# Moving one more batch of output transposes from TensorE to DMA, with a new order of loads and a new rule for the fillers

## The chip, the core and the metric

The kernel runs on one core of one Trainium2 chip. The metric is the device time of that core in microseconds (us), from the first to the last instruction, taken over several executions. Beside each kernel the kernel before was run on the same chip in the same rounds.

PE is the matrix engine (TensorE), ACT is ScalarE, DVE is VectorE, POOL is GpSimd. SP is the engine that issues most of the loads. The granted clock is the share of PE's full clock that it was given in a stretch; 1.00 is full. "PE stands" means that it is idle and waits.

## The reference

The first half is attention with a forget gate; the second half is two linear layers with a SiLU between them.

```python
# q, k, v: (8, 8, 576, 64)   f: (8, 8, 576)   all float32
scores = scale * np.matmul(q, k.transpose(0, 1, 3, 2))
cum = np.cumsum(np.log(np.clip(f, 0.0001, 1.0)), axis=-1)
decay = cum[:, :, :, None] - cum[:, :, None, :]
scores = np.where(causal, -1e9, scores + decay)     # causal: above the diagonal
attn = softmax(scores)                              # max, exp, sum, as usual
x = np.matmul(attn, v) -> (4608, 512)               # 4608 tokens, heads side by side
h = x @ w_in                                        # 512 x 2048
out = (h * sigmoid(h)) @ w_out                      # 2048 x 512
```

## The kernel before

The first 128 tokens of each batch ("heads" of the sequence) are done in an opening phase, batch by batch. Then a loop over 16 pairs of head pairs does the other 448 tokens of each batch. The attention runs ahead; between its steps PE is fed with pieces of the two layers for tokens whose attention is done. A piece of the first layer is `m1_chunk` (line L568, output `hp`), a piece of the second is `m2_part` (L613, output `po`). Between them ACT takes a tanh of `hp` (`th`), and DVE multiplies the two (`gt`, L577): that frees the buffer of `hp`, and `gt` is the input of the second layer. The scores are `sc` (L460). The program sets the order of the instructions on each engine: in the trace of this kernel POOL issues the loads in the program's order, w_out's first two pieces at 25.31 us behind the conversion of v of batch 4 (24.31).

The outputs of PE live in two pools. The scores have one of their own; everything else, `hp`, `po`, the attention outputs `dn` and the transposes `tx`, shares four buffers with the tag "big":

```python
psc = ctx.enter_context(tc.tile_pool(name="psc", bufs=2, space=bass.MemoryType.PSUM))
pbig = ctx.enter_context(tc.tile_pool(name="pbig", bufs=4, space=bass.MemoryType.PSUM))
```

`back(m)` turns (transposes) the attention output of pair-of-pairs m, so that it can be an input of the first layer. It does this by DMA, or by seven transposes on PE and two copies on DVE:

```python
BY_DMA = [2 * 2 <= m < NQ - 1 for m in range(NQ)]        # NQ = 16
def back(m):
    ...
    if BY_DMA[m]:
        nc.sync.dma_start_transpose(out=xr..., in_=xq[:, 0 : 2 * NR, ...])
        nc.sync.dma_start_transpose(out=xt..., in_=xq[:, 2 * NR, ...])
        return
    tx = pbig.tile([P, NGR, P], BF16, name="tx", tag="big")
    for c in range(NGR):                                 # NGR = 7
        nc.tensor.transpose(tx[:, c, :], xq[:, c, ...], ident_bf[:, :])
    nc.vector.tensor_copy(out=xr, in_=...)
    nc.vector.tensor_copy(out=xt, in_=...)
```

`step()` picks the next filler. It compares how far the first layer is in its group of tokens (f1) with how far the second layer is in the group before (f2), and mostly alternates:

```python
f1 = M1[a][1] / NFC
f2 = (c - sum(M2_OF[:g2])) / M2_OF[g2]
want = 3 - at["last"] if abs(f1 - f2) < 0.15 else (1 if f1 < f2 else 2)
if want == at["last"] and at["row"] >= 2 and abs(f1 - f2) < 0.25:
    want = 3 - want
```

The loads of the opening phase are issued by POOL, those of the pair loop by SP. After SP's loads of the first pairs come the cast (on POOL) and the DMA transpose of q and k of pair 0, `qkT`, which the first scores of the pair loop need:

```python
load_qk(2); load_v(0, 2); load_v(0, 3); load_qk(3)       # SP
for n in range(2):
    cast_qk(n)                                           # POOL
    transposes(n)                                        # SP, by DMA: qkT
```

SP's queue has a gate in front of these loads: a tiny DMA into `junk` (the `after(...)` of the kernel), which waits until the second piece of w_out has landed.

The pair loop, cut:

```python
for m in range(NQ):
    scores(n, 0); scores(n, 1); prepare(n)
    slot(piece, 2)                                       # fillers, second layer first
    if m > 0: back(m - 1); ...
    scores(n, 2); scores(n + 1, 0); prepare(n + 1); slot(piece, 2)
    scores(n + 1, 1); scores(n + 1, 2); slot(piece, 2)
    attend(n); attend(n + 1); slot(..., 1)
```

The softmax here doesn't subtract the row's maximum and nothing guards it: scores larger than these inputs give would overflow.

## Time and profile before

| | before |
|---|---|
| median of the runs | 350.6 us (349.71 to 350.83) |
| span of the profiled run | 348.5 us |
| PE busy | 333.4 us, 96% |
| ACT busy | 216.8 us, 62% |
| PE waits for loads of w_out / q | 2.6 us / 1.6 us |
| PE waits for DVE to free a buffer (`po` on `gt`) | 0.9 us |
| PE transposes of attention outputs | 35, in five streams of seven (pair indices 0 to 3, and the last) |

PE is the bound, so the reader looks for two things: what takes PE's time, and where PE stands. The prediction below shows those lines. In the groups of instructions (busy us, mean ns of one, idle before it and what ended most of that):

```profile
L549 PE MATMUL tx<-ident_bf,xr 128*128 128x128 bf16 x35 | 2.8, 219 | 0.2 <-DVE gt L577 0.2
```

In the timeline of PE, start, length, instruction: the first scores of the pair loop start at 62.80 us without a wait.

```profile
62.80 0.40 PE L460 MATMUL sc<-qkT 64*128 64x128 bf16 x8
...
63.35 1.04 PE L613 MATMUL po<-w_out_bf,gt 128*128 128x512 bf16 x4
```

### The profile page before, as it was taken

How to read it: one execution, taken by the hardware profiler on the slowest of the kernel's cores; microseconds unless marked ns; L12 is line 12 of the kernel's file. 1: busy time of each engine (PE TensorE's matmuls, PEld its weight loads, DVE VectorE, ACT ScalarE, POOL GpSimd, SP SyncE). 2: the span in 40 equal slices, each digit the busy share in tenths (PEclk: the TensorE clock that was granted, in tenths of full speed). 3: DMA queues.
4: the chain of work that ended last, by engine and by line, in shares of the span. 5: the costliest groups of instructions: out<-in, count | busy, mean ns of one | idle time of the engine just before them, and what ended most of it. 6: DMA issues, size and time to landing. Idle time of an engine off the chain costs nothing.

```text
span 348.5 us, 8844 instructions
## 1 busy us (share of the span) xinstructions
PE 333.4 (96%) x3520; PEld 199.4 (57%) x3567; DVE 179.4 (51%) x389; ACT 216.8 (62%) x401; POOL 130.0 (37%) x227
## 2 busy tenths in 40 slices
PE   8989969999899999999999999999999999999995
PEld 3644545567656566565665666756656565555664
DVE  4763815366556555645546554645645463444340
ACT  5855624867766758759667585785865934545341
POOL 8997325447271263245235028313620000010011
PEclk9999999999999999999999999999999999999999
DMA  8999999999999398799799789679952100011012
GB/s 155 193 203 207 213 202 184 219 199 188 190 168 187 96 185 165 177 208 163 163 221 137 169 165 194 158 153 197 174 104 58 52 32 30 32 53 40 30 60 62
DMA packets 141497, 50.44 MB, mean 145 GB/s; under 512 B 132368, under 2 KB 138768, under 8 KB 141456
## 3 DMA queue, kind: packets, MB, share of 16 engines
q1 hardware_dynamic: 131440, 32.70, 53.5%
q0 software_dynamic: 9856, 17.04, 20.5%
q8 instruction: 28, 0.46, 0.6%
q10 hardware_dynamic: 160, 0.13, 0.1%
q14 instruction: 13, 0.11, 0.1%
HBM read 36.85 MB, written 9.44 MB: 133 GB/s over the span
## 4 chain that ended last, share of the span: by engine, by line
PE 83%; DMA 6%; ACT 4%; POOL 3%; issue 3%; DVE 1%; ACTq 0%
PE po L613 34%; PE hp L568 29%; PE sc L460 7%; DMA w_out_bf<-in_moe_w_out_dram 6%; PE dn L507 5%; PE dn L516 3%; PE tp L286 2%; PE wm L232 1%; ACT u L464 1%; ACT ut L476 1%; ACT osb L623 1%; POOL qkb L131 1%; PE tx L549 1%; ACT th L576 1%; POOL w_in_bf L190 0%
## 5 line engine op out<-in xcount | busy, mean ns | idle before, releaser
L576 ACT ACTIVATE th<-hp 128x384 bf16<-128x384 f32 (+2 forms) x208 | 95.7, 481 | 88.2 <-PE hp L568 86.3
L577 DVE SCALAR_TENSOR_TENSOR gt<-th,hp 128x384 bf16<-128x384 bf16 (+2 forms) x208 | 105.5, 522 | 82.1 <-ACT th L576 79.0
L613 PE MATMUL po<-w_out_bf,gt 128*128 128x512 bf16 (+1 forms) x550 | 138.7, 373 | 6.7 <-DMA w_out_bf<-in_moe_w_out_dram 2.6
L568 PE MATMUL hp<-x,w_in_bf 128*128 128x384 bf16 (+2 forms) x700 | 129.0, 321 | 0.5
L568 PEld LDWEIGHTS <-w_in_bf 128*128 128x128 bf16 x832 | 78.1, 98 | 53.8 <-issue 1.6
L613 PEld LDWEIGHTS <-gt 128*128 128x128 bf16 x592 | 55.1, 98 | 53.1 <-issue 6.3
L592 POOL DMA_DIRECT2D out_dram<-osb x38 | 21.0, 553 | 170.1 <-ACT osb L623 130.6
L464 ACT ACTIVATE u<-sc 128x1024 bf16<-128x1024 f32 (+1 forms) x96 | 75.2, 822 | 11.9 <-PE sc L460 11.7
L414 POOL TENSOR_TENSOR vp<-vf,w_bf 128x520 bf16<-128x520 f32 (+1 forms) x32 | 35.0, 1100 | 21.2 <-DMA vf<-in_v_dram 14.8
L469 DVE TENSOR_TENSOR u<-u,tri 128x768 bf16<-128x768 bf16 x32 | 20.1, 628 | 24.7 <-ACT u L464 24.7
L623 ACT ACTIVATE osb<-po 128x512 f32<-128x512 f32 (+1 forms) x37 | 22.1, 598 | 14.4 <-PE po L613 14.2
L460 PE MATMUL sc<-qkT 64*128 64x128 bf16 (+1 forms) x640 | 26.5, 207 | 0.1
L460 PEld LDWEIGHTS <-qkT 64*128 64x128 bf16 x640 | 18.2, 94 | 11.8 <-issue 9.3
L483 DVE TENSOR_TENSOR ut<-ut,trit 128x128 bf16<-128x128 bf16 x32 | 8.5, 265 | 30.7 <-ACT ut L476 30.7
L476 ACT ACTIVATE ut<-sc 128x640 bf16<-128x640 f32 x32 | 23.2, 726 | 0.0
L507 PEld LDWEIGHTS <-u 128*128 128x128 bf16 x576 | 20.8, 97 | 3.6 <-issue 0.3
L507 PE MATMUL dn<-vp,u 128*128 128x65 bf16 x384 | 21.8, 193 | 0.0
L525 DVE TENSOR_TENSOR xr<-dn,rec 128x448 bf16<-128x448 f32 x32 | 20.0, 624 | 1.1
L507 PE MATMUL dn<-v,u 128*128 128x65 bf16 x192 | 19.8, 193 | 0.2 <-DVE gt L577 0.2
L400 POOL CAST qkb<-qf 128x384 bf16<-128x384 f32 x32 | 16.2, 508 | 9.2 <-DMA qf<-in_q_dram 8.4
L400 POOL CAST qkb<-kf 128x384 bf16<-128x384 f32 x32 | 18.7, 583 | 2.2 <-DMA kf<-in_k_dram 2.2
L568 PE MATMUL hp<-xt,w_in_bf 128*128 128x256 bf16 x128 | 17.7, 273 | 0.1
(68 smaller groups left out, 204.6 us busy)
## 6 DMA issues: line engine op xcount, KB each, us to landing
out_dram<-osb POOLq DMA_DIRECT2D x32, 256.0 KB, 3.2
vf<-in_v_dram SPq DMA_DIRECT2D x26, 256.0 KB, 4.9
qf<-in_q_dram SPq DMA_DIRECT2D x64, 96.0 KB, 3.0
kf<-in_k_dram SPq DMA_DIRECT2D x64, 96.0 KB, 2.9
w_in_bf<-in_moe_w_in_dram POOLq DMA_DIRECT2D x4, 512.0 KB, 7.2
w_out_bf<-in_moe_w_out_dram POOLq DMA_DIRECT2D x4, 512.0 KB, 10.3
vf<-in_v_dram POOLq DMA_DIRECT2D x6, 256.0 KB, 7.4
qkb<-in_q_dram POOLq DMA_DIRECT2D x8, 128.0 KB, 5.3
```

The lines of the kernel that those rows point to most:

```text
L400: nc.gpsimd.tensor_copy(out=t2[:, c0 : c0 + NR, :].rearrange("p c x -> p (c x)"), in_=t[:, :, :, :].rearrange("p c h d -> p (c h d)"),)
L414: nc.gpsimd.tensor_tensor(out=vbf[b][r, c, :, :], in0=vst[b][c][r, :, :], in1=w_bf[r, c + 1, b * H : (b + 1) * H, None].to_broadcast([n, H ...
L460: nc.tensor.matmul(sc[:, i, o : o + q1 - q0], lhsT=kt, rhs=t[r, q0:q1], start=True, stop=True)
L464: nc.scalar.activation(out=u[:, :, c * SM : c * SM + w], in_=sc[:, :, 0:w], func=ACT.Exp, scale=scale)
L476: nc.scalar.activation(out=ut[:, :, 0:3:2, :].rearrange("p k i t -> p i k t"), in_=sc[:, :, T0 : T0 + (NM + 1) * ST].rearrange("p i (k t) ...
L507: nc.tensor.matmul(dn[:, i * NR + c - 1, :], lhsT=u[:, i, o : o + P], rhs=vals(kb, i), start=(kb == 0), stop=(kb == c),)
L568: nc.tensor.matmul(hp[:, :], lhsT=w_in_bf[:, cc, fc * P : (fc + 1) * P], rhs=xcols(g, cc), start=(cc == 0), stop=(cc == NCC - 1),)
L576: nc.scalar.activation(out=th[:, :], in_=hp[:, :], func=ACT.Tanh, scale=0.5)
L577: nc.vector.scalar_tensor_tensor(out=gt[:, fc, :], in0=th[:, :], scalar=1.0, in1=hp[:, :], op0=ALU.add, op1=ALU.mult,)
L592: q_.dma_start(out=dst, in_=src)
L613: nc.tensor.matmul(po[:, :], lhsT=gt[:, fc, tb * P : (tb + 1) * P], rhs=w_out_bf[:, fc, m0:m1], start=(fc == 0), stop=(fc == NFC - 1),)
L623: nc.scalar.activation(out=osb[:, :], in_=po[:, :], func=ACT.Copy, scale=0.5)
```

## The change

The intent is to take the transposes of the second batch's outputs from PE to DMA (BY_DMA from m = 2 instead of 4). With them come a rule for the fillers and a new order of POOL's loads in two places.

```diff
-    BY_DMA = [2 * 2 <= m < NQ - 1 for m in range(NQ)]
+    BY_DMA = [2 <= m < NQ - 1 for m in range(NQ)]
@@ step()
+            if sum(M2_OF[: g2 + 1]) - c <= 2:
+                want = 1
@@ first part of the load order
     load_qk0(4)
+    load_qk0(5)
+    load_w_in(2)
+    load_w_in(3)
     load_v0(4)
-    load_w_in(2)
-    load_qk0(5)
     load_v0(5)
-    load_w_in(3)
@@ second part of the load order
-    convert_v0(4)
     load_w_out(0)
     load_w_out(1)
+    convert_v0(4)
     convert_v0(5)
-    load_qk0(6)
-    load_v0(6)
-    load_qk0(7)
-    load_v0(7)
     load_w_out(2)
     load_w_out(3)
+    load_qk0(6)
+    load_qk0(7)
+    load_v0(6)
+    load_v0(7)
```

Below, "the rule" is the second of these edits, "the first hunk" and "the second hunk" are the two parts of the load order.

## The prediction

> **What bounds the kernel now.** I read the page first, then the waits of the matrix engine, then stretches of 10 us, then single stretches in order of time.
>
> From the page: busy time of the matrix engine (PE), and two rows of the span in 40 slices (tenths of a slice busy):
>
> ```profile
> span 348.5 us, 8844 instructions
> PE 333.4 (96%) x3520; PEld 199.4 (57%) x3567; DVE 179.4 (51%) x389; ACT 216.8 (62%) x401; POOL 130.0 (37%) x227
> ...
> PE   8989969999899999999999999999999999999995
> ...
> DMA  8999999999999398799799789679952100011012
> ```
>
> PE is the bound: 15.1 us of it idle, and the last slice (the final eviction and store) alone holds about 4. DMA is full from the start to slice 12, some 110 us, then has gaps. So before 110 us PE runs beside a second resource with no reserve.
>
> The waits that PE met (us in total, times, longest):
>
> ```profile
> PE po L613 <- DMA w_out_bf<-in_moe_w_out_dram: 2.6, 2, 1.8
> PE tp L286 <- DMA qkb<-in_q_dram: 1.6, 1, 1.6
> ...
> PE po L613 <- DVE gt L577: 0.9, 1, 0.9
> ```
>
> Only these three are worth more than 0.5 us, apart from the start. The first two are loads that come late. The stretches show where (columns: stretch, its length, then PE busy; last but one is the DMA share):
>
> ```profile
> 20.00:30.00 10.00, 8.32 (x97) 4.34 (x98) 5.58 (x9) 4.02 (x8) 8.35 (x17) 1.00 1.17 210
> 30.00:40.00 10.00, 9.86 (x75) 5.35 (x75) 6.99 (x13) 8.53 (x16) 5.79 (x8) 1.00 1.22 216
> 40.00:50.00 10.00, 7.25 (x43) 4.11 (x43) 3.03 (x8) 2.81 (x7) 2.47 (x5) 1.00 1.05 190
> ```
>
> From 110 to 340 us PE is busy 227.4 of 230 us: there the only gain is less work for PE. The third wait is the one I looked at longest, because it tells what the change's reordering will do. The timeline of PE, then of ScalarE (ACT), then of VectorE (DVE), at 90 to 94 us (start, length, instruction):
>
> ```profile
> 89.86 0.34 PE L460 MATMUL sc<-qkT,kT 64*128 64x384 bf16 x2
> ...
> 90.38 1.92 PE L568 MATMUL hp<-x,w_in_bf 128*128 128x256 bf16 x16
> 93.25 1.02 PE L613 MATMUL po<-w_out_bf,gt 128*128 128x512 bf16 x4 [0.95 <-DVE gt L577]
> ```
>
> ```profile
> 90.50 1.37 ACT L464 ACTIVATE u<-sc 128x1024 bf16<-128x1024 f32 x2
> 91.67 0.80 ACT L476 ACTIVATE ut<-sc 128x640 bf16<-128x640 f32 x1
> 92.25 1.42 ACT L576 ACTIVATE th<-hp 128x256 bf16<-128x256 f32 x4
> ```
>
> ```profile
> 92.77 1.41 DVE L577 SCALAR_TENSOR_TENSOR gt<-th,hp 128x256 bf16<-128x256 bf16 x4
> ```
>
> PE did score matmuls, then four first-layer chunks (16 matmuls) in 1.92 us. ACT had to do the exponentials of those scores before the four tanh, so the first tanh began at 92.25 and the first product on DVE ended at 93.2. The four chunks sat in the four buffers of the pool "big"; the next output needed a fifth, and PE stood for 0.95 us. So: more first-layer chunks in a row behind scores than there are free buffers costs PE about 1 us.
>
> [...] the last two pieces of w_out, issued by POOL at 33.3 and 36.0, took 11.0 and 11.6 us to land, against 7.7 and 9.6 for the first two, with SP's loads starting at 36.4. [...] The trace has 219 ns as duration, but seven in a row start 0.48 us before the next matmuls (86.56 to 87.04), so I count 0.48 us for seven.
>
> **The change part by part.** (1) Two of the sixteen output pairs (the second batch's) leave PE: 2 x 7 transposes = 2 x 0.48 = 1.0 us of PE; on DVE 2 x (0.55 + 0.21) = 1.5 us, beside other work, worth nothing. One of them waited 0.2 us for a buffer at 117.3 (0.23 <-DVE gt): 0.2 more. It adds two DMA transposes of x and two of xt, landing in 3.2 and 2.4 us like the eleven there are. The instruction order puts them in the SP queue near 101 and 112 us, where SP has gaps of some 2 us, and the batch becomes ready one slot later; its first use is near 124 us, so I count 0.
>
> (2) Load order. The q and k of batch 5 go ahead of a v and a piece of w_in, so the 1.58 us wait at 26.7 goes: bytes ahead of it drop by 256 + 512 KB of some 210 GB/s, over 3.5 us. Pieces 2 and 3 of w_out go ahead of q, k, v of batches 6 and 7 (1 MB of destination, about 5 us), so the waits of 0.76 and 1.84 us go. POOL's conversions of v4 and v5 come some 1.5 us later, but I find about 1 us of reserve before their use. Sum: 4.2 us earlier at 50 us.
>
> But the same bytes must land by 60 us. The first transposed q/k of the pair loop is issued by SP at 57.12 behind a full DMA and takes at most 3.3 us: 60.4. PE needs it at 62.80, that is 2.4 us of reserve. PE 4.2 us earlier waits 1.8. The net of (2) is 2.4 us.
>
> (3) The scheduling rule. When two or fewer second-layer parts of a group are left, first-layer chunks go first. The accumulating output then holds one "big" buffer through the whole burst, so only three are left, and the fillers between scores are bunched. I went through the new PE order with measured durations (256 columns: PE 0.43, ACT 0.40, DVE 0.42 us; 384: 0.65, 0.50, 0.55; exponentials of a score group 1.8 to 1.9) and these rules: a chunk needs a free buffer, tanh comes after the exponentials ahead of it on ACT.
> - Third pair (83 to 94 us): 3 chunks, the transposes, scores, 6 chunks of 256. Stalls 0.5 + 1.4 against 1.1 today: +0.8.
> - First tail group: scores, 6 chunks of 256, attention outputs: the fourth chunk waits for the first's product: +1.6. None today.
> - Twice scores, 4 chunks of 384, scores: the fourth waits: 2 x 1.1 = +2.2. None today.
> - Closing stretch, bursts of 6 without scores: a 384 chunk holds its buffer 2.0 us, three buffers give 0.67 per chunk against 0.65: nearly nothing; of 256, 0.5 against 0.43. +0.3, less 0.2 for the last transition.
>
> Sum +4.7. The same method puts the stall at 117.3 at 0.45, where 0.23 was seen, so I take 0.2 off each of four: +3.9.
>
> Total: 350.6 - 1.2 - 2.4 + 3.9 = 350.9. A stall in one place gives the others time, so I say 350.5.
>
> **The rivals.** A, all gains hold and the bursts cost nothing (ACT catches up, or buffers come free sooner): 350.6 - 1.2 - 4.2 - 0.95 = 344.3. For it: PE idle after 110 us is almost nil now, although bursts of 4 chunks are in the order already. Against it: those have four buffers, and the one at 93 us did stall. B, loads gain but the DMA backlog takes nearly all back at 60 us and the bursts are as I count: 352 to 353. For it: DMA share 1.04 over 36 to 110 us. C, only the transposes count, all else shifts within noise: 349. D, the DMA transposes come late for their group and PE runs dry at 120 us, +2 to 4: against it, the same pattern for the later batches shows no idle.
>
> **Range and chances.** Gains between 2 and 6.3 us, burst losses between 0 and 6: 347 to 353.5 eight times in ten. Faster by 2% (under 343.6) needs more than all gains: 0.03. Slower by 2% (over 357.6) needs twice my losses: 0.04.
>
> **What would show it.** In the changed profile: no wait of tp on q, nor of po on w_out; a new wait of the scores or their weight load on the DMA of qkT near 58 to 60 us; waits of hp on DVE gt, 1 to 2 us each, in four places; transposes by PE down from 35 to 21; DMA transposes x and xt 13 each. I am wrong if hp does not wait for gt (then rival A), or if a wait on x or v appears.

## The result

The changed kernel took 355.11 us (353.71 to 356.48 in four runs), the kernel before 350.72 us beside it (349.71 to 351.57). The ratio is 1.0126, with a 95% interval of 1.0078 to 1.0174. All ratios in this document are the mean time of one kernel's runs over the mean of the other's of the same rounds, so they aren't quite the ratios of the medians that are quoted. Executions over 1.5% slower than the fastest of the same kernel are left out of the means. The change is slower, clear of the noise, by less than 2%. The predicted 350.5 and the range up to 353.5 were too low.

The profiled run was the slowest of the four. Its page:

```profile
span 354.7 us, 8820 instructions
...
PE 335.6 (95%) x3506; PEld 199.1 (56%) x3553; DVE 181.1 (51%) x385; ACT 218.8 (62%) x401; POOL 128.6 (36%) x227
...
PEclk9999999699999999999999999999999999999999
```

Two things are odd. PE has 14 matmuls fewer and yet is busy 2.2 us longer (335.6 against 333.4; in both pages the weight loads outnumber the matmuls by 47, 3553 to 3506 and 3567 to 3520, so I take both traces to lack as many matmul records, and compare the two). And the granted clock of PE has a slice of 6 tenths, the eighth, at 62 to 71 us; in it four second-layer matmuls took 1.91 us that took 1.04 before, as the timeline below shows. PE's idle time rose too, from 15.1 to 19.1 us. The waits of PE (total us, times, longest) say where:

```profile
PE sc L460 <- DMA qkT<-qkb: 4.7, 1, 4.7
PE hp L568 <- DVE gt L577: 3.8, 4, 1.3
```

The waits for q, for w_out and of `po` on `gt`, 5.1 us in all before, are gone from the top of this list. In their place stand 8.5 us of new ones: one long wait for the first turned q and k, and four waits of first-layer chunks for a buffer.

The long one in the timeline of PE (the last figure is the idle time before the instruction, with what ended it):

```profile
57.40 0.81 PE L613 MATMUL po<-w_out_bf,gt 128*128 128x512 bf16 x3
62.93 0.61 PE L460 MATMUL sc<-qkT 64*128 64x128 bf16 x8 [4.72 <-DMA qkT<-qkb]
...
66.43 1.91 PE L613 MATMUL po<-w_out_bf,gt 128*128 128x512 bf16 x4
```

PE had done its work at 57.40 + 0.81 = 58.2 us; before, it came to this point at 62.80. So the loads did bring it 4.6 us forward. It then stood for 4.7 us, and began at 62.93, no earlier than before. And then four second-layer matmuls took 1.91 us where they took 1.04 before. The stretches of 2 us show why (columns: stretch, length, PE busy, weight loads, DVE, ACT, POOL, then the granted clock of PE, the DMA share, GB/s):

```profile
60.00:62.00 2.00, 0.00 (x0) 0.00 (x0) 0.00 (x0) 0.00 (x0) 1.05 (x1) 0.94 1.42 112
62.00:64.00 2.00, 1.07 (x13) 0.67 (x14) 0.00 (x0) 0.42 (x1) 0.97 (x3) 0.50 0.74 144
64.00:66.00 2.00, 2.00 (x6) 0.78 (x6) 0.56 (x1) 1.52 (x2) 2.00 (x5) 0.50 0.83 223
66.00:68.00 2.00, 2.00 (x7) 0.76 (x5) 0.42 (x1) 0.38 (x1) 1.06 (x3) 0.50 1.14 224
68.00:70.00 2.00, 1.99 (x29) 1.46 (x30) 0.09 (x1) 1.18 (x3) 0.00 (x0) 0.85 1.08 304
```

The clock halved during the stand and stayed so until about 68.6 us. PE was at half clock for (0.06 + 0.50 x 3 + 0.15) x 2 us / 0.5 = 6.8 us, of which 0.24 + 0.93 us lay in the stand. The other 5.7 us delivered half of their work, so by this estimate the dip cost about 2.8 us in this run. PE counts as busy in it, which is why its busy time rose although it had less to do.

The four waits for a buffer, in the timeline of PE:

```profile
92.97 1.47 PE L568 MATMUL hp<-x,w_in_bf 128*128 128x256 bf16 x12 [1.27 <-DVE gt L577]
...
224.60 1.47 PE L568 MATMUL hp<-xt,w_in_bf 128*128 128x256 bf16 x12 [1.02 <-DVE gt L577]
249.06 0.81 PE L568 MATMUL hp<-x,w_in_bf 128*128 128x384 bf16 x4 [0.78 <-DVE gt L577]
278.67 0.81 PE L568 MATMUL hp<-x,w_in_bf 128*128 128x384 bf16 x4 [0.78 <-DVE gt L577]
```

They are in the places that the prediction named: the third pair, the first tail group, and twice a burst of 384-column chunks between scores.

The transposes that left PE, in the groups:

```profile
L549 PE MATMUL tx<-ident_bf,xr 128*128 128x128 bf16 x21 | 1.7, 219 | 0.3 <-DVE gt L577 0.3
```

35 became 21. The DMA transposes of x and of xt rose from 11 to 13 each, and land in 3.2 and 2.4 us (medians) as before. No wait for them appears among PE's.

The profiled runs differ by 354.7 - 348.5 = 6.2 us. Idle PE explains 4.0 of it, and longer busy time 2.2.

### The profile page after: what moved, and what is told of

It reads as the page before. It is cut to its first block, busy times and chain, and to the rows that moved or that the text cites.

```text
span 354.7 us, 8820 instructions
## 1 busy us (share of the span) xinstructions
PE 335.6 (95%) x3506; PEld 199.1 (56%) x3553; DVE 181.1 (51%) x385; ACT 218.8 (62%) x401; POOL 128.6 (36%) x227
## 4 chain that ended last, share of the span: by engine, by line
PE 75%; DMA 9%; POOL 4%; issue 4%; ACT 3%; DVE 3%; SPq 1%; ACTq 0%; POOLq 0%
PE po L613 31%; PE hp L568 27%; PE sc L460 7%; PE dn L507 5%; DMA kf<-in_k_dram 3%; DMA w_out_bf<-in_moe_w_out_dram 3%; PE dn L516 3%; DVE gt L577 2%; PE wm L232 1%; DMA qkT<-qkb 1%; ACT u L464 1%; SPq L158 1%; DMA vf<-in_v_dram 1%; ACT th L576 1%; POOL v L341 1%
## 5 line engine op out<-in xcount | busy, mean ns | idle before, releaser
L613 PE MATMUL po<-w_out_bf,gt 128*128 128x512 bf16 (+1 forms) x550 | 136.8, 377 | 3.5 <-issue 2.1
L483 DVE TENSOR_TENSOR ut<-ut,trit 128x128 bf16<-128x128 bf16 x32 | 10.6, 330 | 39.0 <-ACT ut L476 39.0
L400 POOL CAST qkb<-qf 128x384 bf16<-128x384 f32 x32 | 17.2, 538 | 21.3 <-DMA qf<-in_q_dram 18.8
L400 POOL CAST qkb<-kf 128x384 bf16<-128x384 f32 x32 | 17.3, 539 | 3.3 <-DMA kf<-in_k_dram 3.2
```

What stands on the lines that cost most here:

```text
L400: nc.gpsimd.tensor_copy(out=t2[:, c0 : c0 + NR, :].rearrange("p c x -> p (c x)"), in_=t[:, :, :, :].rearrange("p c h d -> p (c h d)"),)
L613: nc.tensor.matmul(po[:, :], lhsT=gt[:, fc, tb * P : (tb + 1) * P], rhs=w_out_bf[:, fc, m0:m1], start=(fc == 0), stop=(fc == NFC - 1),)
```

## The experiments

My theory after the result: the transposes gain about 1 us; the loads lose, because PE stands (4.7 us) and then runs at half clock (0.50); the rule loses 3 to 4 us by four waits. The rivals: the loads' gain survives and the rule costs all of it; or the added DMA traffic does the harm. 16 kernels ran (there is no e12), the last four (e14 to e17) because the first twelve left open what made the loads a loss. All gave correct results. Five executions of each were compared with nine or ten of the kernel before.

### Each part alone

`e1_loads_only`: the kernel before, with both hunks of the load order and nothing else.

> The load order alone, on the kernel before. My theory (the loads' gain is given back at the first transposed q/k of the pair loop, and with interest, because PE stands long enough to be run slowly afterwards): no wait of tp or po on loads, a wait of the first scores on the DMA of qkT of 4 to 5 us, PE clock near 0.66 in the stretch from 60 to 70 us, a stall of PE near 93 us as before; 352.5 to 355 us. Rival (the loads are a gain and the rule and the transposes make the changed kernel slow): 346 to 348 us.

`e2_rule_dma`: the change with the load order of before.

> The rule and the DMA transposes, with the loads of before. My theory (bursts behind scores cost 4 us in four stalls, the transposes give 1.0, the stall at 93 us of before, 0.95, and the one at 117, 0.23, go or are counted in the bursts): waits of hp on DVE gt of about 3.8 us in four places, full clock throughout, 351.5 to 353. Rival (the four stalls are only the echo of the late start and vanish with it): under 350.

`e3_dma_only`: the kernel before, with this alone:

```diff
-    BY_DMA = [2 * 2 <= m < NQ - 1 for m in range(NQ)]
+    BY_DMA = [2 <= m < NQ - 1 for m in range(NQ)]
```

> The second batch's transposes by DMA alone, loads and rule of before. My theory: 14 transposes less on PE (1.0 us), no new wait: 349 to 350.5. Rival (the batch becomes ready a slot later, PE runs out of first-layer work near 100 to 125 us and the rule was put in to mend that): a wait of PE there, 351 to 354.

`e4_rule_only`: the kernel before, with the two lines of the rule alone.

> The rule alone. My theory: stalls of hp or tx on DVE gt, 3 to 4 us, against 1.2 before: 352.5 to 354.5. Rival (the rule costs nothing by itself): 350 to 351.

| | median, us | before beside it | ratio | 95% interval |
|---|---|---|---|---|
| e1_loads_only | 351.6 | 350.49 | 1.0041 | 1.0007 to 1.0076 |
| e2_rule_dma | 353.32 | 350.49 | 1.0084 | 1.0054 to 1.0113 |
| e3_dma_only | 349.56 | 350.49 | 0.9985 | 0.9951 to 1.0018 |
| e4_rule_only | 354.21 | 350.49 | 1.0115 | 1.0076 to 1.0153 |

The parts add up: +0.41% for the loads and +0.84% for rule and DMA make 1.25%, and the whole change has 1.26%. In microseconds of 350.5 that is +1.4 and +2.9. The rule alone costs +4.0. The transposes gain nothing that is clear of the noise by themselves (the median is 0.9 us lower). The times of e1 (below the range that I gave) and e2 (just above) were missed: the loads cost less, and rule and DMA a little more, than I expected. So the rival "the rule costs all of it" falls, since the loads lose by themselves, and the rival "the added DMA traffic" falls with e3.

The waits of PE in e4 show that the rule carries the same waits as the whole change:

```profile
PE hp L568 <- DVE gt L577: 3.9, 4, 1.3
```

The loads alone show the same stand as the whole change, and the same dip. Timeline of PE and stretches in e1:

```profile
61.61 0.40 PE L460 MATMUL sc<-qkT 64*128 64x128 bf16 x8 [3.13 <-DMA qkT<-qkb]
```

```profile
62.00:64.00 2.00, 2.00 (x12) 0.82 (x7) 0.56 (x1) 1.94 (x2) 2.00 (x6) 0.61 0.59 133
64.00:66.00 2.00, 2.00 (x8) 0.76 (x5) 0.42 (x1) 0.38 (x1) 1.72 (x5) 0.54 1.02 210
66.00:68.00 2.00, 2.00 (x29) 1.13 (x28) 0.23 (x1) 1.47 (x3) 0.00 (x0) 1.00 1.09 334
```

Here the stand was shorter, and PE was still 62.80 - 61.61 = 1.2 us ahead of before when it ended. The clock was full at that moment and fell only about 0.8 us later; the dip (0.39 + 0.46) x 2 us / 0.5 = 3.4 us long cost 1.7 us, and the lead was gone. This profiled run ended 0.5 us later than the profiled run of before (349.0 against 348.5), which is 1.7 - 1.2.

The mean granted clock of whole executions agrees. A dip as long as that of e1's profiled run, 3.4 us at half clock, takes 1.7 / 350 = 0.005 from the mean. The means of these executions lie near such steps:

| kernel | mean granted clock of its runs, fastest run first |
|---|---|
| the change | 0.995, 0.990, 0.995, 0.990 |
| e1_loads_only | 0.995, 0.995, 0.994, 0.990, 0.990 |
| e2_rule_dma | 0.999, 0.999, 0.999, 0.998, 0.993 |
| e5_warm (next section) | 0.999, 1.000, 0.997, 1.000, 0.999 |

By this estimate each run of the change and of e1 had one or two dips of that length, and in e1 the two runs with two are the slowest. With the old order most runs of e2 had none.

### The stand and the clock

`e5_warm`: the change, with 16 matmuls on zeros ahead of the first scores of the pair loop. PE has to wait for `qkT` as before, but is busy for most of that time.

```diff
     for m in range(NQ):
+        if m == 0:
+            keep_warm(16)
         scores(n, 0)
```

> The changed kernel with 16 matmuls of 512 columns on constant data (3.5 us of PE) put ahead of the first scores of the pair loop, where PE stands for 4.7 us. They compute nothing that is used. My theory (that stand costs twice: 4.7 us of waiting, then about 2.7 us because PE runs at half its clock for some 5 us after it): wait about 1.2 us, PE clock 1.00 in the stretch from 60 to 70 us, 2 to 3 us faster than the changed kernel, so 352 to 353. Rival (the low clock is an echo of the wait and costs nothing, since DMA sets the time there): 355 as the changed kernel.

It took 353.05 us (352.79 to 353.38), ratio 1.0076 (1.0046 to 1.0106): 2.1 us less than the change. In its waits and in its stretch of 10 us:

```profile
PE sc L460 <- DMA qkT<-qkb: 1.0, 1, 1.0
```

```profile
60.00:70.00 10.00, 9.04 (x105) 5.18 (x104) 2.44 (x7) 6.55 (x12) 4.62 (x10) 1.00 0.93 201
```

The clock stays at 1.00 where the change had 0.66 over the same 10 us. The data still came late (the scores began at 62.43 us, against 62.93 in the change's profiled run), so what this run took away is mainly the dip: 2.1 us on the median, of which up to 0.5 us can be the earlier landing. This is the term that was missing in my prediction.

`e6_turn_early`: the change, with the cast and the turn of pairs 0 and 1 moved ahead of loads that they don't need. SP then issues the DMA transpose of pair 0 before the loads of v and of pair 3.

```diff
     load_qk(2)
+    cast_qk(0)
+    transposes(0)
     load_v(0, 2)
     load_v(0, 3)
+    cast_qk(1)
+    transposes(1)
     load_qk(3)
-    for n in range(2):
-        cast_qk(n)
-        transposes(n)
```

> The changed kernel, but the two DMA transposes of the first q/k pairs stand earlier in the SP queue: the first behind the loads of the third pair, the second behind the rest of v, both ahead of the fourth pair's loads. Theory (the first scores wait because these transposes stand last in a queue whose loads land one after another, not because the casts are late): they land 3 to 5 us earlier, the wait of 4.7 us goes below 1.5, the clock stays at 1.00, 347.5 to 350; the four stalls of hp on gt stay at 3.8. Rival (DMA as a whole sets the time and the wait moves to another tile): a new wait of scores or attention of several us, 352 to 355.

353.13 us (352.28 to 353.74), ratio 1.0072 (1.0043 to 1.0101). The wait for `qkT` fell to 1.0 us in all, the four waits of the rule stayed (3.9 us). Its profiled run also stood 1.3 us for w_in in the opening phase (of the others only e14 did, 0.9 us), so I lean on the times only. They miss the 347.5 to 350 that I expected: the early turn gained no more than the warm PE of e5 (353.05). Part of the rest can be what the timeline of e7 below shows, waits that move to later pairs.

`e7_turn_early_norule`: the same without the two lines of the rule.

> As the last, without the rule: the loads' order and DMA transposes of the change, the earlier turn. Theory: the rule's stalls go too (3.8 us, against 1.2 to 2 that the old order has), so 345 to 347 and faster than before by more than 1%. Rival (what is gained until 60 us is lost to later waits on DMA): 348.5 to 351.

348.74 us (347.87 to 349.47), before 350.76; ratio 0.9946 (0.9916 to 0.9975). This beats the kernel before by half a per cent. I had expected 345 to 347; the time is in the rival's range. Taking the rule away from e6 was worth 4.4 us.

`e9_turn_early_loads`: the load order and the early turn alone, with neither the rule nor the new BY_DMA.

> The loads' order with the earlier turn alone; transposes on PE and scheduling as before. Theory: the loads' gain of 4.2 us is then kept: 346 to 348. Rival: 350 to 351.5, as with the loads' order alone.

349.25 us (348.57 to 352.21), ratio 0.9988 (0.9946 to 1.0031). So without the late `qkT`, the load order no longer loses, but it doesn't gain the 4 us that I expected either. The timeline of PE in e7 shows where the rest goes:

```profile
73.31 0.40 PE L460 MATMUL sc<-qkT 64*128 64x128 bf16 x8 [0.75 <-DMA qkT<-qkb]
...
81.81 0.40 PE L460 MATMUL sc<-qkT 64*128 64x128 bf16 x8 [1.60 <-DMA qkT<-qkb]
```

The first scores no longer wait, and those of later pairs wait instead, 2.4 us in all (3.0 in e9). DMA was full there (share 1.33 in e7 from 70 to 80 us), and part of the lead is taken back a little later.

### Which half of the load order

`e8_first_hunk`: the kernel before, with the first hunk alone.

> The first half of the loads' order alone (q and k of batch 5 ahead of v and w_in), on the kernel before. Theory: the wait of tp on q (1.6 us) goes, the waits on w_out stay, and PE is early at the pair loop by less than the 2.4 us of reserve there, so nothing is given back: 348.5 to 349.5. Rival (any earlier arrival is given back there): 350 to 351.

356.25 us (354.81 to 357.08), ratio 1.0166. This edit was badly made. The first hunk puts `load_v0(4)` later, and `convert_v0(4)` still stood ahead of `load_w_out(0)` in POOL's order, so POOL waited for v (landed at 29.7 us) before it issued w_out at 30.8. DMA moved 0 to 30 GB/s from 30 to 33 us (128 GB/s over 30 to 40 us, against 216 before). PE then stood 5.5 us for w_out, and the clock dipped (0.87 over 40 to 50 us, 0.78 over 50 to 60). The run shows how the two hunks depend on each other, and says nothing of the first by itself.

`e10_second_hunk`: the kernel before, with the second hunk alone.

> The second half alone (two pieces of w_out ahead of q, k, v of batches 6 and 7). Theory: the waits of po on w_out (2.6 us) go, the first turned q/k lands 1 to 2 us later than before since this half makes the queue's tail and the first loads of SP end later, so the first scores wait 1 to 2.5 us: 350 to 351.5. Rival (the first half is what delays it): no wait of the scores, 348 to 349.

349.16 us (348.67 to 350.25), before 350.12; ratio 0.9978 (0.9954 to 1.0002), so lower than before, but not clear of the noise, and better than I expected. PE comes to the first scores at 61.57 - 1.82 = 59.75 us, 3.0 us earlier than before in place of 4.6, since it still waits for q (1.3 us). The stand is shorter:

```profile
61.57 0.40 PE L460 MATMUL sc<-qkT 64*128 64x128 bf16 x8 [1.82 <-DMA qkT<-qkb]
```

The clock stays full here (1.00 in all stretches of 2 us from 56 to 72 us). When the stand ends, this kernel is 62.80 - 61.57 = 1.2 us ahead of before, just as e1 was. It keeps that lead, and e1 lost it to the dip: the smaller gain upstream gives the better kernel.

`e13_first_hunk_dma_turn`: the first hunk, the new BY_DMA and the early turn.

> The best of the parts without the second half: first half of the loads' order, second batch's transposes by DMA, the earlier turn of the first pairs, no rule. Theory: 1.6 + 1.0 us less, the waits on w_out stay (2.2 us), the waits of scores on qkT that both halves with the earlier turn have at 73 and 82 us (2.4 us) are under 1: 347.5 to 348.7, near the 348.7 of that one. Rival (DMA takes back the same, whichever wait of PE is removed): 349.5 to 350.5.

352.81 us (352.47 to 355.96), ratio 1.0101. It has the same fault as e8 (5.4 us of waits for w_out), so my expectation was missed for a reason that it didn't test.

`e15_first_clean`: the first hunk mended. `convert_v0(4)` moves behind the two loads of w_out, and the tail of the order stays as before.

```diff
-    convert_v0(4)
     load_w_out(0)
     load_w_out(1)
+    convert_v0(4)
     convert_v0(5)
```

> The first half of the loads' order alone, with the conversion of v of batch 4 behind the first two pieces of w_out as the change has it (without that, POOL waited for v before it issued them, and the DMA queue ran dry for some 4 us: PE waited 5.5 us on w_out). Theory: the wait on q goes, waits on w_out of 2 to 3.5 us stay, the first turned q/k lands at 59.6 to 60.8, no wait at the first scores: 348.5 to 350. Rival (this half delays the first turned q/k): landing over 61.5 and a wait there, 350.5 to 352.

350.96 us (349.78 to 352.81), before 349.81; ratio 1.0038 (1.0001 to 1.0076). The wait for q is gone, but a wait moves:

```profile
PE po L613 <- DMA w_out_bf<-in_moe_w_out_dram: 5.0, 2, 2.9
```

The last pieces of w_out are used at 44.5 and 48.0 us; PE only comes to them sooner. Of the two hunks, the first is worth nothing without the second. The first turned q and k landed at 60.6 us, as my theory had it; the time is the rival's, because the wait for w_out grew. Two of its five runs also had a mean clock of 0.990, by the estimate above two dips; the profiled run had 1.000.

`e16_first_clean_dma`: e15 with the new BY_DMA.

> The last with the second batch's transposes by DMA: 0.9 us less, as that part gave alone: 347.8 to 349.2. Rival: the same as the last or slower, 349.5 or more.

350.68 us (349.43 to 351.64), ratio 1.0013 (0.998 to 1.0047): no different from before, and not the gain that I expected. Its profiled run shows that the length of a stand alone doesn't decide about the clock. Timeline of PE and stretches, e15 first, then e16:

```profile
44.51 1.02 PE L613 MATMUL po<-w_out_bf,gt 128*128 128x512 bf16 x4 [2.94 <-DMA w_out_bf<-in_moe_w_out_dram]
44.00:46.00 2.00, 1.46 (x8) 0.78 (x8) 0.00 (x0) 0.00 (x0) 0.00 (x0) 1.00 1.21 201
```

```profile
44.43 1.82 PE L613 MATMUL po<-w_out_bf,gt 128*128 128x512 bf16 x4 [2.51 <-DMA w_out_bf<-in_moe_w_out_dram]
44.00:46.00 2.00, 1.57 (x4) 0.55 (x4) 0.00 (x0) 0.00 (x0) 0.00 (x0) 0.63 1.21 196
```

The stand of 2.94 us in e15 (and one of 2.1 us after it) left the clock at 1.00; after 2.51 us in e16 it was halved for 6.8 us.

`e17_second_dma`: the second hunk and the new BY_DMA, without the first hunk and without the rule.

> The second half of the loads' order with the second batch's transposes by DMA, no rule: 349.2 less 0.9, so 347.8 to 348.8 and faster than the kernel before; a wait of 1 to 2 us at the first scores. Rival: no gain over the second half alone, 349 or more.

348.42 us (348.09 to 349.97), before 349.81; ratio 0.9964 (0.9936 to 0.9992). With e7 it is the best of the kernels that ran. Its stand for `qkT` is 1.6 us, and the clock does not dip in the stretches around it (1.00 from 56 to 72 us).

### Two tests of the explanations

`e11_rule_four`: the rule alone, with a threshold of 4 in place of 2.

```diff
-            if sum(M2_OF[: g2 + 1]) - c <= 2:
+            if sum(M2_OF[: g2 + 1]) - c <= 4:
```

Four parts make one block of 128 tokens. With 2, a half-done `po` is open and holds a buffer while the burst runs; with 4 the burst starts before it is opened. If the held buffer makes the waits, they should shrink.

> The rule alone with a threshold of 4 parts in place of 2. The parts of one output tile are four, so at four left no output tile is open and a burst of first-layer chunks has all four buffers, not three. Theory (the stalls come from a buffer held open behind ACT's exponentials): waits of hp, tx or po on DVE gt fall from 4.2 us to about 2, from more than one place still, as one burst of 5 and one of 6 chunks of 256 columns follow scores; 351.5 to 353, against 354.2 with two. Rival (the number of buffers has nothing to do with it): 4 us and 354 as before.

353.85 us (352.03 to 357.7; the highest is not in the ratio), ratio 1.0091 (1.0062 to 1.012). The waits moved to other instructions and did not shrink: 4.4 us in place of 3.9.

```profile
PE dn L507 <- DVE gt L577: 2.5, 6, 0.8
...
PE hp L568 <- DVE gt L577: 1.9, 2, 1.2
```

So freeing the held buffer, which my prediction named, doesn't cure them, and the waits and the time are the rival's. The bursts got longer in this edit, too (in the closing stretch eight chunks in a row where e4 has six), so it doesn't show that the held buffer plays no part. What both versions share is the bunching: a row of chunks behind the exponentials of a score group, whose tanh on ACT comes late, so that their buffers come free late. That this is the whole cause is argued, not shown.

`e14_v_first`: e1 with the loads of v of batches 6 and 7 ahead of w_out, so that none of v's small rows are left at the end of POOL's queue when SP's loads start. It tests why `qkT` of pair 0 lands later with the second hunk.

```diff
+    load_v0(6)
+    load_v0(7)
     load_w_out(2)
     load_w_out(3)
     load_qk0(6)
     load_qk0(7)
-    load_v0(6)
-    load_v0(7)
```

> The loads' order alone, but v of batches 6 and 7 ahead of the last two pieces of w_out, so that the queue's tail is q and k (rows of 2 KB) in place of v (rows of 256 bytes). Theory (small rows of v beside SP's small rows are what slows the tail): the first turned q/k lands at 60 to 60.8, the first scores wait 1 to 2 us, not 3.1, the last w_out pieces make PE wait under 1 us; 349 to 350.5, against 351.6. Rival (it is enough that v or q/k instead of w_out stand at the tail, or that PE's issue of SP's queue sets it): landing at 61.5 to 62.9 and 351 to 352.5.

351.98 us (350.01 to 352.53), ratio 1.0048 (1.0016 to 1.008): no better than e1, and `qkT` of pair 0 landed at 62.8 us. The small rows of v are not the cause. This run adds one point on the clock:

```profile
62.84 0.40 PE L460 MATMUL sc<-qkT 64*128 64x128 bf16 x8 [2.73 <-DMA qkT<-qkb]
```

After a stand of only 2.7 us the clock fell, 0.8 us after PE had begun again, for 3.4 us.

### What stays open

What decides about the clock after a stand is open. In the profiled runs it fell with stands of 2.5 us (e16), 2.7 us (e14), 3.1 us (e1) and 4.7 us (the change), to 0.63, 0.50, 0.54 and 0.50 in the lowest stretch of 2 us looked at. In the first three it fell 0.1 to 0.8 us after PE had begun again; in the change it fell in the stand, 3.6 us after its beginning. It stayed at 1.00 with stands of 1.6 and 1.8 us (e17, e10), and with one of 2.9 us (e15).

In the kernels with POOL's old tail of loads (before, e2, e3, e4, e11, e15, e16), `qkT` of pair 0 landed between 59.6 and 61.2 us. With the second hunk (the change, e1, e5, e10, e14, e17) it landed between 61.5 and 62.9. It was issued at nearly the same time in both, at 56.5 to 57.9 and at 56.4 to 58.4 us; it took 3.1 to 3.5 us to land in the first group and 4.4 to 5.1 us in the second. The small rows of v are excluded as the explanation (e14: 62.8 us without them at the tail). The order of the tail isn't the whole of it either: e13 has the old tail, and its turn took 4.4 us (57.4 to 61.8).

The DMA side of the traces gives a lead. In all seven traces in which this turn took 4.4 us or more, DMA nearly stops for some 1 us before it lands: under 40 GB/s in the emptiest half microsecond, where the eleven other traces have at least 70 up to the landing. Stretches of half a microsecond in the change, then around the landing (60.4) in the kernel before; the last two columns are the DMA share and GB/s:

```profile
60.50:61.00 0.50, 0.00 (x0) 0.00 (x0) 0.00 (x0) 0.00 (x0) 0.50 (x1) 1.00 1.40 57
61.00:61.50 0.50, 0.00 (x0) 0.00 (x0) 0.00 (x0) 0.00 (x0) 0.05 (x1) 1.00 0.08 18
```

```profile
59.50:60.00 0.50, 0.50 (x12) 0.45 (x9) 0.47 (x3) 0.00 (x0) 0.50 (x1) 1.00 0.39 78
60.00:60.50 0.50, 0.50 (x5) 0.26 (x3) 0.50 (x2) 0.31 (x1) 0.14 (x1) 1.00 1.10 210
```

In the same seven a packet of 16 KB in the DMA queue of kind "instruction" starts between the issue and the landing (at 58.4 us in the change); in the eleven others none does (in the kernel before it starts at 62.3, after the landing). The change from 58 to 59 us (packets, MB, share of 16 engines):

```profile
q8 instruction: 1, 0.02, 8.5%
```

With PE earlier, this packet comes earlier, too, and so may meet the loads. No run moves it by itself, and most such packets (384 of the 504 in the 18 traces) are not followed by a stop within 2.5 us, so that it is the cause is not shown.

## Why the prediction was wrong, and where it was right

- **The transposes (step 1): right in kind, and hardly measurable.** I predicted 1.2 us of gain, from the trace of before: one PE transpose has a duration of 219 ns there, and seven in a row hold PE for 0.48 us (86.56 to 87.04). Alone they gave 0.9 us on the median (e3), with an interval that includes none. PE transposes fell from 35 to 21 and no wait for the DMA transposes came in, as predicted.
- **The loads, first half of step 2: right.** I predicted that PE comes 4.2 us earlier. It came to the first scores of the pair loop 4.6 us earlier, and the waits for q and w_out were gone.
- **The loads, second half of step 2: this is the step that failed.** "The first transposed q/k of the pair loop [...] takes at most 3.3 us: 60.4 [...] PE 4.2 us earlier waits 1.8. The net of (2) is 2.4 us." The wait existed, in the place named, but it was 4.7 us. The landing that I took over from the old order, 60.4, became 62.9: the turn was issued 1.0 us later (58.16) and took 4.7 us. My "at most 3.3" came from the first two turns; a third one in the same trace, issued at 61.80, took 5.9. And a term was missing altogether: with the stand PE lost half its clock (0.50), for 6.8 us in the profiled run of the change and for 3.4 us in that of e1, worth about 2.8 and 1.7 us there. The net of the loads was a loss of 1.4 us (e1), in place of a gain of 2.4: an error of 3.8 us, and the whole miss is 355.1 - 350.5 = 4.6 us. What made the turn slower stays open.
- Knowledge of this term would not have been enough: my wait was 1.8 us, and e10 and e17, with stands of 1.8 and 1.6 us, kept a clock of 1.00. The mis-sized wait had to come first.
- **The rule (step 3): right in its places, and in its total partly by luck.** The predicted 3.9 us were what the waits would grow by, and the rule alone cost 4.0 us on the ratio (e4). But the four waits sum to 3.8 us, and the 0.9 us at 93 us of the kernel before are gone, so they grew by 2.9 us. Each was shorter than I had worked out: 1.27, 1.02, 0.78 and 0.78 us, against 1.7, 1.4, 0.9 and 0.9 with the 0.2 us taken off. The remaining 1 us of e4 is not in these waits, and no run places it. Rule and transposes together, predicted at 3.9 - 1.2 = +2.7 us, measured +2.9 (e2). My reason for the waits was half tested: in e11 they stayed although there, by the order of the program, no `po` is open when such a burst begins.
- The prediction sets the landings of the last two pieces of w_out in the kernel before (11.0 and 11.6 us) beside the start of SP's loads (36.4). Such landings come without SP's loads, too: in the change the first two pieces took 9.4 and 11.1 us, and they landed (33.5 and 35.9) before SP's loads began (36.6).
- **The rivals.** B, in which the loads' backlog takes nearly all back, came closest with 352 to 353, and is still 2 us too low: it let the stand take back the gain, and nothing more. A, C and D are out: there are waits of `hp`, the time did not fall, and PE did not run dry at 120 us.

## What to carry to other kernels

In this kernel a wait removed early was only worth the reserve of the next hand-over that depends on something else, here a DMA transpose near 60 us; look up that reserve, and don't assume that its data still land at the old time once the loads ahead of it are reordered (60.4 us became 62.9 here). The stands of PE of 2.5, 2.7, 3.1 and 4.7 us (e16, e14, e1, the change) cost more than their length, because the clock fell with them (to 0.50 in the change); with one of 2.9 us (e15) it stayed at 1.00. Matmuls that filled most of the stand gave 2.1 us (e5), and a smaller gain upstream (e10, e17: 0.9978 and 0.9964) was better than a larger one that ended in a longer stand (e1: 1.0041). When a change bundles several edits, try the parts and leave one out: the transposes and one half of the loads gain 0.4% (e17), or the whole of both with the turn moved up 0.5% (e7), once the rule is gone.
